# Recurrence and feed-forward on one core: output tiles of their own, more transposes by DMA, and a written order for every step

## The chip, the cores and the metric

The kernel runs on one core of a Trainium2 chip. The metric is the device time of one execution in microseconds (us). Three runs of the kernel before gave 186.01, 186.14 and 186.18 us; the median is 186.14 us.

## What is computed

The reference has two parts. The first is a recurrence with decay over 768 positions, for 4 batches x 8 heads, with head size 48. All inputs are float32.

```python
for t in range(S):
    cur = np.einsum('bhd,bhe->bhde', u[None] * kt, vt)
    y[:, :, t] = np.einsum('bhd,bhde->bhe', rt, state + cur)
    state = wt[:, :, :, None] * state + np.einsum('bhd,bhe->bhde', kt, vt)
```

The second takes y as a matrix x of 3072 rows and 384 columns and computes `h = x @ w_in` (384 x 2048), `g = max(0.01 h, h)` and `g @ w_out` (2048 x 384).

## The kernel before, in words

The 3072 rows are cut into 24 chunks of 128 positions, six for each batch. The recurrence is turned into matrix products inside a chunk, with a state carried from chunk to chunk inside a batch. Chunks 0 to 3 are done as two pairs (`pair`), whose rows are dealt out alternately so that a load moves runs of 384 bytes; the other twenty one at a time (`single`), in runs of 192 bytes.

For a single chunk the steps are these. Four loads bring w, k, r and v (192 KB each) into a quarter each of a tile `in` (L516). ACT takes the logarithm of w (`lw`, L383). PE forms its cumulative sum in PSUM (`cp`, L737) and the decay of the whole chunk (L742). DVE adds one row (`ci`, L752); ACT takes exponentials (L393). DVE or POOL multiply r and k by them and write bfloat16 (`rk`, L334). r and k are then transposed into `rkT`, in `turn`: either eight PE transposes into PSUM (L441) and two copies, or one DMA transpose issued by SP (L431). PE computes the scores (`se`, `so`, L787), DVE masks them (`m`, L459), and PE sums the part from the state (L817) and the part within the chunk (L822) into `yp`. The bonus for u is made apart: POOL multiplies r by u and by k (`ru`), DVE sums over a head (`dg`, L416), POOL multiplies v by that (`vs`). In `finish` DVE adds `yp` and `vs` into y (L490), and y is transposed into a slice of `xT`: by three PE transposes (L504) and a copy, or by a DMA transpose on SP (L496). The state goes on through an outer product (L798), a sum (L479) and a product with the decay (`sb`).

The feed-forward part works chunk by chunk on `xT`. An up group is 12 matmuls into one of two PSUM banks `hp` (L860); ACT applies the leaky function and writes a quarter of `g` (L907). A down group is 4 matmuls into a bank `op` (L928), which needs one quarter of `g` and one quarter of `w_out`. After four down groups ACT or DVE copies `op` to a tile `o` (one of four), and SP stores it (L968). The last chunk is computed in two column parts, 256 and 128 wide (L928 and L940), which are copied and stored apart (L952).

The weights come as 16 halves of 384 KB (L363), each of which is cast to bfloat16 (L329 or L331) by DVE, ACT or POOL. They pass through the same ring of 11 `in` tiles as the chunks' inputs.

The order of the work is set at build time. Each step is added to a `Plan` with an engine, a duration and its dependencies. `EARLY` ranks the steps by hand, with letters that move some to another engine; `Plan.order` then plays a schedule by priorities and gives the sequence in which instructions are issued. Every engine then works strictly in its own sequence. All loads, stores and DMA transposes are issued by SP, in one queue; only the row u is fetched by ACT. While little has arrived, PE is fed matmuls on zeros (L991).

Of the kernel before, what the change touches and what calls it, by code (L numbers as in the profile page):

```python
# [2 lines left out]

# [9 lines left out]
AX = mybir.AxisListType  # L13


class Plan:
# [23 lines left out]
    def order(self):  # L40
        n = len(self.eng)
        users = [[] for _ in range(n)]
        left = [len(d) for d in self.deps]
        for i, d in enumerate(self.deps):
            for j in d:
                users[j].append(i)
        ready_at = [0.0] * n
        start, done = [None] * n, [0.0] * n
        free = {e: 0.8 for e in self.ENGINES}
        coming = {e: [] for e in self.ENGINES}  # L50
        ready = {e: [] for e in self.ENGINES}
        dma_free = 0.0
        flying = []
        for i in range(n):
            if not left[i]:
                heapq.heappush(coming[self.eng[i]], (0.0, i))
        events = [(0.8, e) for e in self.ENGINES]
        heapq.heapify(events)
        count = 0
        while events:  # L60
            now, e = heapq.heappop(events)
            if free[e] > now + 1e-9:
                continue
            while coming[e] and coming[e][0][0] <= now + 1e-9:
                _, i = heapq.heappop(coming[e])
                heapq.heappush(ready[e], (self.pri[i], i))
            if not ready[e]:
                if coming[e]:
                    heapq.heappush(events, (coming[e][0][0], e))
                continue  # L70
            _, i = heapq.heappop(ready[e])
            start[i] = now
            count += 1
            free[e] = now + self.dur[i] * (1.8 if e == "PE" and now < 8 else 1)
            if self.wire[i] is None:
                done[i] = free[e] + self.LAT[e]
            else:

                flying = [x for x in flying if x[0] > free[e]]
                while sum(x[1] for x in flying) + self.rows[i] > 3300:  # L80
                    free[e] = max(free[e], flying.pop(0)[0])
                dma_free = max(dma_free, free[e]) + self.wire[i]
                done[i] = dma_free + 1.7
                flying.append((done[i], self.rows[i]))
            heapq.heappush(events, (free[e], e))
            for j in users[i]:
                left[j] -= 1
                same = self.eng[j] == e and self.wire[i] is None
                ready_at[j] = max(ready_at[j], free[e] if same else done[i])
                if not left[j]:  # L90
                    f = self.eng[j]
                    heapq.heappush(coming[f], (ready_at[j], j))
                    heapq.heappush(events, (max(ready_at[j], free[f]), f))
        assert count == n, (count, n)
        self.start, self.done = start, done
        return sorted(range(n), key=lambda i: (start[i], i))


class Ring:
# [7 lines left out]
    def take(self):  # L107
        self.n += 1
        k = self.n % len(self.tiles)
        old, self.steps[k] = self.steps[k], []  # L110
        return Use(self.tiles[k], old, self.steps[k])

# [14 lines left out]
def kernel(  # L127
# [24 lines left out]
    TDMA = range(12, NCH)  # L152
# [4 lines left out]
    PWIRE, WIRE, WWIRE = 1.53, 1.15, (1.12, 1.12)  # L157
# [4 lines left out]
    EARLY = """  # L162
        0 4 2 1 3 5 8 58 7 13 6 61 12 32v 36 17 11 16 22 33 120 14 21 30 19 37 18 20 24 15 59 10a 23 26
        9 27 31v 28 40 25 60 29a 38 41a 51 34 39 63 44 53 114 62 42 116 45 65a 66 118 121 64 67 122 46
        35 43 71 68 124 47 126 52 74 73 69 96 48 70 128 76 49 75p 72 136 50v 132 79 115a 78 54 91 80 81
        117 130 83 55 77p 82v 56 84a 721 119 134 92 57 85 722 723 86v 138 87 123a 93 95 725 724 97 125p
        98v 727 726 146 127p 729 99 728 88v 100 129 94 731 89 730 102 137p 140 732 733 101 735 133 148
        90 103 734 131 107 736 104 741 135p 144 109 105 742 106v 139a 142 747 108 737 147 150 110 738
        152 141p 178 743 111 153 112 748 304 744 162 113v 754 167 166 155 168 145v 749 154 753 156 750
        143p 149 739 158 163v 179 157p 755 740 759 164 756 180 160 159 182 762 760 184 209 306 745 763v  # L170
        161 185 765 764 746 151v 169 181 187 165v 751 199 761 189p 198 186 170 171 766 752 172 768 302
        173 757 208 188 174 758 192 210 200v 770 193 774 175 183a 239 194v 190 176 775 767 191a 195v 769
        211 177 196 201 779 197 202 212 237 777 780 203 214 771 224 271 778 215 204 217 781 225v 253 303
# [90 lines left out]
    with tc.manual_schedule():  # L264
# [52 lines left out]
        def step(eng, dur, fn, pri, reads=(), writes=(), deps=(), wire=None, rows=0, **alts):  # L317
# [5 lines left out]
            for x in (*reads, *writes):  # L323
                x.steps.append(i)
            return i

        def copy(e, o, i):
            if e == "ACT":
                nc.scalar.copy(out=o, in_=i)  # L329
            else:  # L330
# [697 lines left out]
```

## Time and profile before

| | |
|---|---|
| profiled execution | 186.2 us, with a span of 184.1 us |
| median of three runs | 186.14 us |
| PE busy | 175.5 us (95% of the span), 2579 matmuls |
| PE weight loads busy | 136.5 us (74%) |
| DVE busy | 121.8 us (66%), 237 instructions |
| ACT busy | 121.5 us (66%), 263 instructions |
| POOL busy | 93.4 us (51%), 129 instructions |
| DMA queue of SP and ACT | 34.22 MB in 120208 packets, 84.6% of 16 engines |
| from HBM, to HBM | 25.17 MB, 4.72 MB |
| stores of 192 KB | 23, median 3.2 us from issue to landing |
| DMA transposes of r and k | 12, median 4.2 us from issue to landing |
| DMA transposes of y | 12, median 2.6 us from issue to landing |

The profile is of one execution, so sums of its durations are to be set against its own 186.2 us. The 2.1 us beside the span lie around it. A PE that shows as busy is not a PE at its pace, since matmuls are pipelined and their ends are modelled; the distance from one group's start to the next one's is the better price. In the timeline a line gives the start, the time until the last instruction's end, engine, line, operation, tiles and count, and in brackets the idle time before it and what ended it. SPq stands for SP's queue of transfers, and PEld for the weight loads of PE. In the stretches each engine's busy time is followed by its count of instructions; the last three columns are granted clock, DMA share and GB/s.

### The profile page before, as it was taken

What the parts mean: (1) busy time and instruction counts of PE and PEld (TensorE: products, weight loads), DVE (VectorE), ACT (ScalarE), POOL (GpSimd) and SP (SyncE); (2) the same over time, 40 slices, a digit from 0 to 9 for tenths busy, and PEclk for the clock granted to TensorE, in tenths of its full rate; (3) what the DMA queues carried; (4) which work ended last, traced back from release to release, by engine and by line L of the source; (5) the groups of instructions that cost most, each with busy time, mean ns of one, the idle gap of its engine ahead of it and who ended that gap; (6) DMA issues with size and microseconds to landing.
All of it is one profiled execution on the core that took longest, in us unless ns stands there. A gap on an engine that the chain in (4) does not pass through costs nothing.

```text
span 184.1 us, 6227 instructions
## 1 busy us (share of the span) xinstructions
PE 175.5 (95%) x2579; PEld 136.5 (74%) x2583; DVE 121.8 (66%) x237; ACT 121.5 (66%) x263; POOL 93.4 (51%) x129
## 2 busy tenths in 40 slices
PE   7977799999999999999999999999999999999992
PEld 2455587877788687789687787886968777877882
DVE  2498585468679878987968768557548588755000
ACT  2784875666787887698957586766657645652660
POOL 7987582552566778789065667313516346110000
PEclk9999999999999999999999999999999999999999
DMA  6999999999999899996885997988989997641202
GB/s 150 261 282 319 348 331 275 266 180 219 221 185 232 167 234 200 227 206 151 174 155 103 135 196 152 212 166 174 191 196 192 169 183 206 162 115 33 66 4 85
DMA packets 120238, 34.62 MB, mean 188 GB/s; under 512 B 109841, under 2 KB 120210, under 8 KB 120210
## 3 DMA queue, kind: packets, MB, share of 16 engines
q1 hardware_dynamic: 120208, 34.22, 84.6%
q8 instruction: 20, 0.33, 0.7%
q14 instruction: 8, 0.07, 0.1%
q10 hardware_dynamic: 2, 0.00, 0.0%
HBM read 25.17 MB, written 4.72 MB: 162 GB/s over the span
## 4 chain that ended last, share of the span: by engine, by line
PE 82%; SPq 10%; DMA 5%; ACT 1%; issue 0%; DVE 0%
PE op L928 34%; PE hp L860 33%; SPq L363 5%; DMA in<-in_moe_w_out_dram 5%; SPq L516 4%; PE se L787 3%; PE yp L822 2%; PE cp L737 2%; PE yp L817 2%; PE yp L798 2%; PE so L441 1%; PE yp L504 1%; PE se L441 1%; PE cp L742 1%; ACT g L907 1%
## 5 line engine op out<-in xcount | busy, mean ns | idle before, releaser
L907 ACT ACTIVATE g<-hp 128x512 bf16<-128x512 f32 x96 | 56.8, 596 | 35.3 <-PE hp L860 33.4
L860 PE MATMUL hp<-xT,w_in_b 128*128 128x128 bf16 x1152 | 76.2, 219 | 1.4 <-ACT w_in_b L329 0.9
L860 PEld LDWEIGHTS <-w_in_b 128*128 128x128 bf16 x1152 | 67.4, 98 | 6.4 <-ACT w_in_b L329 1.2
L928 PE MATMUL op<-w_out_b,g 128*128 128x384 bf16 (+1 forms) x380 | 71.4, 324 | 0.2 <-ACT g L907 0.2
L928 PEld LDWEIGHTS <-g 128*128 128x128 bf16 x392 | 34.8, 98 | 17.8 <-DVE w_out_b L331 0.3
L334 POOL TENSOR_TENSOR ru<-in,ub 128x384 f32<-128x384 f32 x19 | 19.1, 1010 | 11.7 <-DMA in<-in_r_dram 8.1
L334 POOL TENSOR_TENSOR rk<-in,ek 128x384 bf16<-128x384 f32 x15 | 15.6, 1038 | 17.2 <-ACT ek L393 15.9
L334 POOL TENSOR_TENSOR vs<-in,dg 128x384 f32<-128x384 f32 x19 | 16.2, 855 | 14.2 <-DVE dg L416 11.1
L490 DVE TENSOR_TENSOR y<-yp,vs 128x384 bf16<-128x384 f32 x24 | 13.3, 554 | 13.1 <-PE yp L822 9.6
L334 POOL TENSOR_TENSOR ru<-ru,in 128x384 f32<-128x384 f32 x15 | 15.6, 1043 | 3.9 <-DMA in<-in_k_dram 2.3
L334 POOL TENSOR_TENSOR sb<-s,a 128x384 bf16<-128x384 f32 x13 | 11.3, 867 | 11.9 <-DVE s L479 5.1
L459 DVE TENSOR_TENSOR m<-se,maskb 128x512 bf16<-128x512 f32 x20 | 13.7, 684 | 3.6 <-PE so L787 3.3
L459 DVE TENSOR_TENSOR m<-so,maskb 128x512 bf16<-128x512 f32 x20 | 13.7, 684 | 3.2 <-PE so L787 3.2
L383 ACT ACTIVATE lw<-in 128x384 bf16<-128x384 f32 x24 | 12.3, 519 | 3.3 <-DMA in<-in_w_dram 3.3
L334 DVE TENSOR_TENSOR rk<-in,cp 128x384 bf16<-128x384 f32 x22 | 12.0, 547 | 3.1 <-ACT cp L393 2.1
L752 DVE TENSOR_TENSOR ci<-cp,lw 128x384 f32<-128x384 f32 x20 | 11.1, 553 | 3.8 <-PE cp L742 3.5
L416 DVE TENSOR_REDUCE dg<-ru 128x8 f32<-128x384 f32 x24 | 13.0, 544 | 0.2
L329 ACT COPY o<-op 128x384 f32<-128x384 f32 (+1 forms) x16 | 7.5, 471 | 6.5 <-PE op L928 5.1
L479 DVE TENSOR_TENSOR s<-yp,sb 128x384 f32<-128x384 f32 x14 | 7.8, 554 | 5.2 <-PE yp L798 4.3
L393 ACT ACTIVATE cp<-cp 128x384 f32<-128x384 f32 x22 | 10.5, 478 | 0.6 <-DVE ci L752 0.3
L393 ACT ACTIVATE ek<-ci 128x384 f32<-128x384 f32 x20 | 10.4, 518 | 0.4 <-DVE ci L752 0.2
L787 PE MATMUL se<-rkT 48*128 48x128 bf16 x80 | 7.9, 219 | 0.0
(125 smaller groups left out, 220.7 us busy)
## 6 DMA issues: line engine op xcount, KB each, us to landing
out_dram<-o SPq DMA_DIRECT2D x23, 192.0 KB, 3.2
in<-in_w_dram SPq DMA_DIRECT2D x20, 192.0 KB, 4.0
in<-in_r_dram SPq DMA_DIRECT2D x20, 192.0 KB, 3.8
in<-in_k_dram SPq DMA_DIRECT2D x20, 192.0 KB, 3.8
in<-in_v_dram SPq DMA_DIRECT2D x20, 192.0 KB, 3.8
in<-in_moe_w_in_dram SPq DMA_DIRECT2D x8, 384.0 KB, 7.6
in<-in_moe_w_out_dram SPq DMA_DIRECT2D x8, 384.0 KB, 7.5
in<-in_w_dram SPq DMA_DIRECT2D x2, 384.0 KB, 5.0
```

The costliest lines, as they stand in the source:

```text
L334: (nc.vector if e == "DVE" else nc.gpsimd).tensor_tensor(out=o, in0=a, in1=b, op=ALU.mult)
L363: "SP", 0.45, lambda part=part, src=src: nc.sync.dma_start(out=part, in_=src), pri,
L383: lambda: nc.scalar.activation(out=lw.t[:, :, 0:D], in_=wn.t, func=AF.Ln),
L393: "ACT", 0.5, lambda: nc.scalar.activation(out=out.t[:], in_=i, func=AF.Exp, scale=scale),
L416: lambda: nc.vector.tensor_reduce(out=dg.t[:], in_=ru.t[:], axis=AX.X, op=ALU.add),
L459: lambda par=par: nc.vector.tensor_tensor(out=m.t[:, par], in0=gt(sc[par].t), in1=mask.unsqueeze(1).to_broadcast([128, NP, 128]), op=ALU.m ...
L490: lambda: nc.vector.tensor_tensor(out=y.t[:], in0=hd(yp.t[:, 0:DM]), in1=vs.t[:], op=ALU.add),
L752: lambda: nc.vector.tensor_tensor(out=ci.t[:], in0=hd(cp.t[:, 0:DM]), in1=lw.t[:, :, 0:D], op=ALU.add),
L787: nc.tensor.matmul(gt(sc[par].t)[:, p, :], lhsT=rkT.t[q0 : q0 + D, NP + p, :], rhs=rkT.t[q0 : q0 + D, p, :], start=True, stop=True, skip_g ...
L860: nc.tensor.matmul(hp.t[:, a * N : (a + 1) * N], lhsT=w_in_b[:, t, (j + a) * 128 : (j + a + 1) * 128], rhs=xT[:, t, c0 : c0 + N], start=(a ...
L907: lambda hp=hp, g=g, j=j, J=J, N=N: nc.scalar.activation(out=g.t[:, j : j + J, 0:N], in_=hp.t[:, 0 : J * N].rearrange("p (a n) -> p a n", ...
L928: nc.tensor.matmul(t[:, 0 : n1 - n0], lhsT=g.t[:, j, off : off + 128], rhs=w_out_b[:, j, n0:n1], start=(j == 0), stop=(j == NJ - 1))
```

## The change

DMA transposes of r and k begin at chunk 9 instead of 12, and those of y at chunk 6. Weight casts of w_in get an access pattern whose outer dimension is 2 instead of 3. Outputs of chunks 4 to 23 no longer turn through four `o` tiles: chunks 0 to 3 keep one each, and the others get a quarter each of the `in` tiles 6 to 10, which the weights have left. So single chunks turn through six `in` tiles (1 to 5, and 0). Stores of chunks up to 20 rank behind the loads. Loads of single chunks and stores may be issued by ACT as well as SP; the new order has ACT issue five loads and two stores. The last chunk's down groups are regrouped: all of the 256-wide part's first three quarters, then the 128-wide part's first two, its rest at the very end. `EARLY` and the schedule by priorities go: `ORDER` lists every step once, in the sequence in which it is issued, with letters (a, v, p, s) for the engine. `Plan.order` only reads it and reckons times for the matmuls on zeros. Some reckoned durations of steps differ; they have no other effect. The core of the diff:

```diff
-    def order(self):
+    def order(self, words):
+
+        order = []
+        for word in words.split():
+            i = int(word.rstrip("avps"))
+            if word[-1] in "avps":
+                self.eng[i] = {"a": "ACT", "v": "DVE", "p": "POOL", "s": "SP"}[word[-1]]
+                self.dur[i] = self.alts[i][self.eng[i]]
+            order.append(i)
...
+    def use(self, k):
+
+        return Use(self.tiles[k], list(self.steps[k]), [])
...
-    TDMA = range(12, NCH)
+    TDMA = range(9, NCH)
+    YDMA = range(6, NCH)
+    OLATE = 21
...
-    EARLY = """
...
+    ORDER = """
...
     in_r = ring("in", 11, [128, 1536], F32)
+    pair_slots = iter((0, 1, 2, 3))
+    weight_slots = iter((4, 5, 6, 7, 8, 9, 10, 0))
+    chunk_slots = cycle((1, 2, 3, 4, 5, 0))
...
+    def out_tile(ch):
+
+        if ch < 4:
+            return o_r.take()
+        slot, i = divmod(ch - 4, 4)
+        use = in_r.use(6 + slot)
+        return View(use, use.t[:, i * DM : (i + 1) * DM])
...
+        def queue(e):
+            return nc.sync if e == "SP" else nc.scalar
...
+        def even(t, which):
+
+            return t if which else t.rearrange("p t (a f) -> p a t f", a=2)
...
-            st = in_r.take()
+            st = in_r.take(next(weight_slots))
...
-                    lambda e, dst=dst, part=part: copy(e, dst, part), CASTS, reads=[st], deps=[ld],
-                    DVE=0.8, ACT=0.84, POOL=1.2))
+                    lambda e, dst=even(dst, which), part=even(part, which): copy(e, dst, part),
+                    CASTS, reads=[st], deps=[ld], DVE=0.63, ACT=0.84, POOL=0.84))
...
-            if n in TDMA:
+            if n in YDMA:
                 xt_steps.append(step(
...
-                "SP", 0.45, lambda: nc.sync.dma_start(out=view(use), in_=src), P0 + 0.1 * i,
-                writes=[use], wire=wire, rows=1024, deps=[cums[n - AHEAD]] if n >= AHEAD else [])
+                "SP", 0.62, lambda e="SP": queue(e).dma_start(out=view(use), in_=src), P0 + 0.1 * i,
+                writes=[use], wire=wire, rows=1024, deps=[cums[n - AHEAD]] if n >= AHEAD else [],
+                **({"SP": 0.62, "ACT": 0.47} if n >= 4 else {}))
...
-            slot = in_r.take()
+            slot = in_r.take(next(chunk_slots))
...
+        def quarters(op, g, off, which):
+            for part, q in which:
+                t, n0, n1 = last_parts(op)[part]
+                for j in range(q * NJ // 4, (q + 1) * NJ // 4):
+                    nc.tensor.matmul(
+                        t[:, 0 : n1 - n0], lhsT=g.t[:, j, off : off + 128], rhs=w_out_b[:, j, n0:n1],
+                        start=(j == 0), stop=(j == NJ - 1))
...
+                    if last:
+                        quarters(op, g, off, ((0, q),) if q < 2 else ((0, 2), (1, 0), (1, 1)))
+                        return
...
-                        o = o_r.take()
...
+                        o = o_r.take() if part else out_tile(ch)
+                        s_dn = step(
+                            "PE", (0.44, 0.46)[part],
+                            lambda op=op, g=g, off=off, qs=(((0, 3),), ((1, 2), (1, 3)))[part]: quarters(op, g, off, qs),
+                            pri, reads=[g, op, side], deps=deps)
...
-                    o = o_r.take()
+                    o = out_tile(ch)
...
-                        lambda o=o, ch=ch: nc.sync.dma_start(
+                        lambda e, o=o, ch=ch: queue(e).dma_start(
                             out=rows[ch], in_=o.t[:]),
-                        5, reads=[o], deps=[s_o], wire=0.55, rows=128)
+                        5 if ch >= OLATE else 300, reads=[o], deps=[s_o], wire=0.55, rows=128, SP=0.48, ACT=0.47)
...
-        for i in plan.order():
+        for i in plan.order(ORDER):
```

## The prediction, made before the changed kernel was run

> **What bounds the kernel now.** I read the slices of the span first, then the stretches, the timeline of PE, the casts of the weights, and the chain's end.
>
> ```profile
> PE   7977799999999999999999999999999999999992
> DMA  6999999999999899996885997988989997641202
> ```
>
> PE is full from slice 7 (28 us) to the last slice. DMA is full up to about 80 us, has room after it and much at the end.
>
> ```profile
> 0.00:28.00 28.00, 22.82 (x377) 15.16 (x381) 18.01 (x45) 18.59 (x37) 21.67 (x49) 1.00 1.08 283
> 28.00:170.00 142.00, 141.82 (x2068) 112.21 (x2066) 103.26 (x191) 96.75 (x216) 71.77 (x81) 1.00 0.88 183
> ```
>
> The second column is PE: 141.82 of 142 us, while DVE, ACT and POOL have slack. A busy PE need not be a PE at its pace, so I took the pace from starts in the timeline of PE:
>
> ```profile
> 65.63 0.39 PE L441 MATMUL se<-ident,rk 128*128 128x128 bf16 x4
> 65.85 0.81 PE L928 MATMUL op<-w_out_b,g 128*128 128x384 bf16 x4
> 66.50 1.50 PE L860 MATMUL hp<-xT,w_in_b 128*128 128x128 bf16 x24
> 67.84 0.33 PE L817 MATMUL yp<-sb,rkT 128*128 128x96 bf16 x4
> ...
> 69.35 0.33 PE L504 MATMUL yp<-ident,y 128*128 128x128 bf16 x3
> 69.52 0.33 PE L928 MATMUL op<-w_out_b,g 128*128 128x384 bf16 x1
> ```
>
> From start to start: four transposes of r or k cost 0.22 us, three of y 0.17, an up group (12 matmuls) 0.67, a down group (4) 0.65. The same reading gives the scores of a chunk 0.32, the cumulative sum 0.27, the outer product 0.17, and the two parts of y 0.17 and 0.20. I put these prices on every group of PE's instruction list, leaving out the matmuls on zeros: the real work is **163.0 us** in the list of before and **160.7 us** in that of after. Clock minus work done so far is the time lost. At L737's groups before it is 15.1 us (33.3 us on the clock), 15.2 (40.3), 16.2 (90.0), 17.3 (148.6), and 17.85 when PE ends at 180.85. So 15 us are lost in the first 33 us, and then only some 0.12 us per chunk, which I take for what my prices miss. PE has no stall worth having after 33 us: the time is start-up, PE's work, and the tail.
>
> The start-up is set by weights coming in. Their casts on POOL, ACT and DVE start as the halves land, each after a wait for its DMA:
>
> ```profile
> 26.47 0.82 POOL L331 CAST w_out_b<-in 128x768 bf16<-128x768 f32 x1 [0.40 <-DMA in<-in_moe_w_out_dram]
> ```
>
> ```profile
> 27.64 0.83 ACT L329 CAST w_out_b<-in 128x768 bf16<-128x768 f32 x1 [0.59 <-DMA in<-in_moe_w_out_dram]
> 31.31 0.83 ACT L329 CAST w_out_b<-in 128x768 bf16<-128x768 f32 x1 [1.85 <-DMA in<-in_moe_w_out_dram]
> ```
>
> Others start at 28.84 (DVE), 30.11 and 33.05 (POOL), 35.91 (DVE). So a half lands each 1.17 us, and 31.31 to 33.05 and 33.05 to 35.91 hold one small load each (192 KB): 1.74 - 1.17 = 0.57, and 2.86 - 2.34 = 0.52. A small load among them costs **0.55 us**.
>
> **What the Trainium skill says.** "TensorE: Matmul & The Clock Gate", section "Wait — 56ns, not 53.3ns?", gives a warm matmul N / 2.4 GHz plus about 2.5 ns, 55.6 ns for 128 columns: the trace agrees, 0.67 us / 12 = 56 ns. "DMA: Bandwidth & Descriptors", section "Issuing engines are not separate DMA queues", says that transfers issued by ACT run on the same 16 engines and save only issue time; before, ACT issues one tiny transfer, so the trace is silent. "VectorE: DVE Perf Modes", section "What auto-detection actually checks", wants outermost dimensions that are both even for the fast copy of one source: the trace agrees, 0.95 us for the DVE cast of w_in with an outer 3, and 0.56 for w_out with an outer 4 (once 0.83).
>
> **The change, part by part.**
>
> *Transposes off PE.* r and k of chunks 9, 10, 11: 3 x 2 x 0.22 = 1.32 us. y of chunks 6 to 11: 6 x 0.17 = 1.02 us. All lie in the full stretch: **-2.34 us**. With them go their PSUM copies (6 at 0.41 to 0.59, 6 at 0.36 to 0.48 us on ACT and DVE), nothing on the path.
>
> *What takes their place.* Nine DMA transposes more on SP. An issue holds SP for 1.2 us (y) or 1.2 to 3.1 (r and k, median 1.54), and landing takes a median of 2.6 and 4.2 us from the issue. Nothing waits long if PE has other work. In PE's list of after, y to its first up group is 5.4 to 10.0 us apart for chunks 9 to 20 and 5.9 to 7.3 for chunks 6 to 8 (needed: DVE 0.55, landing 2.6, some 0.2 of latency: 3.3). Cumulative sum to scores is 8.8 us at the least (chunk 23) and 9.5 to 16 otherwise; needed are 0.25, 0.55 (DVE), 0.5 and 0.5 (ACT), 0.55 and 0.65 to 1.04 (products), then 4.2, in all about 7.5 us. Before has 8.1 at chunk 23 and does not stall. Cost 0, with about 1 to 2 us of cover at chunks 11, 12, 17, 18, 22 and 23; a landing of 5.5 (the longest seen) would cost some tenths.
>
> *Stores behind loads, a tile each.* Before the last load 13 stores are issued instead of 19, so 6 x 192 KB make room for nine transposes (3 x 256 KB, 6 x 96 KB). DMA's share of 0.88 between 28 and 170 us stays about the same. Six stores now stand in SP just ahead of the transpose of chunk 22: at 0.35 to 0.55 each some 3 us of queue, for which the list leaves 16 us from cumulative sum to scores. Cost 0. The loads of chunks 4 on turn in six buffers instead of eleven; each load is held until the fifth chunk before has its sum anyway. Cost 0; if late readers held a buffer, a load would slip by the time of one bonus product on POOL (1.0 us), under the same cover.
>
> *Start-up order.* This has a price. The first down group now comes after 12.0 us of work (before: 14.5), and its two halves of w_out are SP's transfers 16 and 17 (before: 18 and 19). Transfer 17 landed at 26.47 before, with the same bytes ahead. So the cast ends at about 27.1, and the first down group can start some 2 us before the old 29.47. But work moved behind it too, so what counts is the loss. Following each wait with the rows of before: the two halves for up group 1 land at 18.5 and 19.64, and POOL's second cast ends near 20.5; ACT's copy of y (0.48), of keys (0.58) and g (0.60 each) follow one another, and the first down group starts at about 27.4, a loss of 15.4. Then two loads of chunk 5 issued by ACT (right after the fifth and sixth g, near 27.2 and 28.0) and one of chunk 4 go ahead of w_out's last halves. Second quarter: 26.47 + 3 x 1.17 + 2 x 0.55 = 31.1, POOL 0.83 and latency: 32.0, where PE wants it at 31.4. Third quarter: 31.1 + 0.55 + 3 x 1.17 = 35.1, ACT 0.83: 36.05, at 19.8 us of work: a loss of **16.25 us**. Fourth: 36.3, POOL to 37.2, work 21.96: no wait. Before had lost 15.15 there: **+1.1 us**. Bounds: -0.3 (ACT's loads fall behind the weights, 2 x 0.55, and a cast or two is quicker) to +1.9 (each of the three small loads costs 0.93 us, the pace between 40 and 80 us at 207 GB/s, and a g is late by 0.5).
>
> *Even casts.* One DVE cast of w_in falls from 0.95 to about 0.56; ACT and POOL keep 0.83. It waits for a landing and has slack: 0.
>
> *ACT issues five loads and two stores.* At about 0.5 us each, 3.5 us of ACT that had 45 us idle in the full stretch; behind each are g's, and PE has two hp banks. In the lists every transfer waits for the one issued eight before it, on whichever queue; those before ACT's loads are old. Cost 0, at worst one g late by 1 us or so each time.
>
> *Tail.* Before, PE ends at 180.85, DVE's copy takes 0.29, two stores are issued one after the other, and the span ends 3.25 us after PE. After, the 128 KB store is ready 1.7 us early, the 64 KB one stands alone on SP, and ACT sends another of 192 KB. I take 3.0: **-0.25**, bounds -0.5 and +0.3.
>
> **Sum.** -2.34 + 1.1 - 0.25 = -1.5 us. The profiled execution took 186.2 (span 184.1 and 2.1 around it), 0.06 above the median of 186.14. So 186.2 - 1.5 = **184.7 us**.
>
> **Rivals.** (a) *The start-up loses nothing more*: ACT's loads fall in a hole, and the whole of PE's saving shows: 186.2 - 2.34 - 0.25 = 183.6; down to 182.9 where the earlier down groups fill time that was lost. For it: DMA moved 266 to 348 GB/s in this stage, so there is some room. (b) *The saving is hidden or given back*: the weights take all of 1.9 us, or one late transpose 1 us, and 186.2 stands. Against: PE is full after 33 us. (c) *Slower: SP's queue becomes the bound.* 33 transposes instead of 24 stand in order with the loads, and each that waits for its product holds up all behind it. Place: chunks 11, 12, 17, 18, 22, 23, where cover is 1 to 2 us. Price: an issue of 3.1 instead of 1.5 and a landing of 5.5 instead of 4.2 make 2.9 us, 1.4 beyond a cover of 1.5. Two such come to 2.8: 184.7 + 2.8 = 187.5. It decides from 1.9 us of PE stalls on. For it: SP waited for products of DVE and POOL up to 3.6 us at a time before; against: that never stalled PE.
>
> **Chances.** Below 183.2: 0.06. Rival (a), 183.2 to 184.2: 0.24. The forecast, 184.2 to 185.75: 0.45. Rival (b), 185.75 to 186.5: 0.09. Rival (c): 0.16. About 0.2% (0.37 us) is what measuring this kernel can tell from no change. Faster 0.75, same 0.09, slower 0.16. The range leaves out 0.06 below and some 0.14 above: 183.2 to 186.6.
>
> **What would show it.** Right: 42 fewer transposes on PE, PE full from about 36 us on, the loss near 16.2 us at the fourth w_out quarter and growing by 0.12 per chunk, POOL and ACT waiting for w_out until about 31, 35 and 36 us, span near 182.6. Wrong: scores (L791) or up groups (L864) waiting for a DMA in mid-span, ACT idle behind its own loads, g late, or a tail above 3.5 us.

## The result, and the profile after

The changed kernel takes **191.85 us** (median of four runs, 190.54 to 193.25), the kernel before 186.16 (186.01 to 186.41) in the same comparison: a ratio of 1.031, with a 95% interval from 1.023 to 1.038. It is slower by 5.7 us. In some of the kernels below, single executions lie more than 1.5% above the fastest of the same kernel; the medians count them, the ratios leave them out. The forecast of 184.7 and its range to 186.6 were wrong; the nearest rival was (c), slower through SP's queue, at 187.5. The profiled execution of the changed kernel took 192.25 us, with a span of 189.9.

The slices of the span, after (each column is 4.75 us):

```profile
PE   7988779899999999999997899999999899999992
PEclk9999999999999999999999699999999999999999
DMA  6999999998996898999999968989999998941302
```

PE, full before from slice 7 on, now has a hole in slices 22 and 23 (100 to 109 us), with a lower granted clock in the second, and a small one in slice 32 (147 to 152 us). With the prices of the forecast put on the 160.7 us of real work in after's list, the loss (clock minus work) reads at the cumulative sums, L741: 17.82 us at chunk 5 (43.05 on the clock), 19.14 at chunk 14 (89.41), 21.79 at chunk 15 (105.11), 23.43 at chunk 16 (113.00), 24.04 at chunk 21, 24.99 at chunk 22 (150.34), and 25.65 when PE ends at 186.31. Against before's losses (15.21 at chunk 5, 17.85 at the end) the span's 5.8 us come out as follows: PE's work -2.34, start-up +2.61, from there to PE's end +5.19 (4.05 of it from chunk 14's sum to chunk 16's, 0.83 from chunk 21's to chunk 22's), tail +0.34 (3.59 us from PE's end to the span's, before 3.25).

The chain of what ended last, after, through the hole (start, us, what):

```profile
96.88 2.39 SPq L434
99.27 0.04 issue
99.31 0.58 SPq L519
...
99.99 4.52 DMA in<-in_w_dram
104.51 0.02 issue
104.53 0.53 ACT lw L386
105.06 0.04 issue
105.11 0.32 PE cp L741
105.43 0.08 PE cp L746 x4
105.51 2.09 PE hp L864 x24
```

PE waited for the sum of chunk 15 (L741), that for ACT's logarithm, that for the load of w, and the load for its turn on SP, behind the transposes. Two up groups then took 2.09 us, where 1.34 is usual: the second part of the loss, 1.64 us, is a lower clock. This is one execution: in the profile of stores_last, below, every engine has the same sequence up to 106.30 us, and yet the loss at chunk 15 is 1.9 us smaller and the clock doesn't fall. What two profiles differ by at this place is therefore no sure sign of an edit. SP's queue in the timeline, after:

```profile
89.00 2.71 SPq L499 DMA_TRANSPOSE xT<-y  x1
91.75 0.58 SPq L519 DMA_DIRECT2D in<-in_v_dram  x1
92.44 1.72 SPq L434 DMA_TRANSPOSE rkT<-rk  x1
94.20 0.58 SPq L519 DMA_DIRECT2D in<-in_k_dram  x1
94.89 1.20 SPq L499 DMA_TRANSPOSE xT<-y  x1
96.13 0.58 SPq L519 DMA_DIRECT2D in<-in_r_dram  x1
96.88 2.39 SPq L434 DMA_TRANSPOSE rkT<-rk  x1
99.31 0.58 SPq L519 DMA_DIRECT2D in<-in_k_dram  x1
99.99 0.53 SPq L519 DMA_DIRECT2D in<-in_w_dram  x1
```

and before, in the same stretch:

```profile
84.90 1.36 SPq L431 DMA_TRANSPOSE rkT<-rk  x1
86.31 0.57 SPq L516 DMA_DIRECT2D in<-in_r_dram  x1
86.93 0.63 SPq L516 DMA_DIRECT2D in<-in_k_dram  x1
89.39 0.36 SPq L968 DMA_DIRECT2D out_dram<-o  x1
89.79 0.43 SPq L516 DMA_DIRECT2D in<-in_k_dram  x1
91.50 1.24 SPq L431 DMA_TRANSPOSE rkT<-rk  x1
```

Before has holes of 1.8 and 1.3 us ahead of 89.39 and 91.50; after has none. Added up over the timeline (gaps under 0.2 us closed), SP is taken 11.3 of the 20 us from 80 to 100 before, and 20.0 of 20 after. Each transpose of y of chunks 8 to 13 is issued 1.1 to 2.7 us after its y is done. The DMA engines are busier there too. The stretch from 80 to 100 us, before and then after (the last three columns are granted clock, DMA share, GB/s):

```profile
80.00:100.00 20.00, 20.00 (x300) 15.91 (x298) 16.03 (x31) 15.80 (x40) 12.34 (x15) 1.00 0.77 157
```

```profile
80.00:100.00 20.00, 19.80 (x291) 15.69 (x290) 16.20 (x33) 12.79 (x29) 9.98 (x12) 1.00 1.07 159
```

The same 157 to 159 GB/s, but a share of 1.07 in place of 0.77. (The share adds up the time that packets took, and these times overlap: it reaches 1.35 between 104 and 106 us. So a share of 1 is no ceiling.) The DMA queues of after (q1 is SP's; q10 is ACT's, with its seven transfers of 192 KB):

```profile
q1 hardware_dynamic: 120384, 34.22, 86.9%
q10 hardware_dynamic: 5490, 1.38, 3.3%
```

90.2% of 189.9 us is 171.3 us of packet time; before it was 84.6% of 184.1, 155.7 us. The nine transposes add 1.38 MB (4%), and the packet time grows by 15.6 us (10%). The trace's packets tell the two parts of it apart by size, for only transposes have packets of 256 bytes (1024 of them for r and k, 384 for y). Their sum over 16 engines goes from 25.0 to 34.3 us: +9.3 are more transposes. The 192-byte packets of the loads are as many as before and take 16.9 ns each in place of 15.7: +5.7 us are the same loads, slowed. From 80 to 100 us they take 20.9 ns.

The start-up, after, on POOL, ACT and DVE:

```profile
33.63 0.83 POOL L330 CAST w_out_b<-in 128x768 bf16<-128x768 f32 x1 [1.78 <-DMA in<-in_moe_w_out_dram]
```

```profile
36.74 0.83 ACT L328 CAST w_out_b<-in 128x768 bf16<-128x768 f32 x1 [1.76 <-DMA in<-in_moe_w_out_dram]
```

```profile
24.27 1.00 DVE L330 CAST w_in_b<-in 128x768 bf16<-128x768 f32 x1 [1.16 <-DMA in<-in_moe_w_in_dram]
25.18 0.54 DVE L482 TENSOR_TENSOR s<-se,sb 128x384 f32<-128x384 f32 x1
```

The cast of w_out's third quarter begins at 36.74, with the landing; forecast 35.1. The casts before it were at 31.02 and 33.63, so the two small loads that ACT sent stretched the landings by 33.63 - 31.02 - 1.17 = 1.44 and 36.74 - 33.63 - 2.34 = 0.77 us, where I had 0.55 each. And DVE waited for a half of w_in with its sums of the state behind it; PE waited 1.2 us for such a sum until 27.25.

### The profile page after: what moved, and what is told of

Same layout as the page of the kernel before. It is cut to its first block, busy times and chain, and to the rows that moved or that the text cites. A ratio compares the mean times of both kernels' runs of the same rounds, so it can differ in the third digit from the quotient of the medians.

```text
span 189.9 us, 6143 instructions
## 1 busy us (share of the span) xinstructions
PE 177.7 (94%) x2546; PEld 137.4 (72%) x2546; DVE 119.2 (63%) x229; ACT 114.4 (60%) x250; POOL 100.6 (53%) x138
## 3 DMA queue, kind: packets, MB, share of 16 engines
q10 hardware_dynamic: 5490, 1.38, 3.3%
## 4 chain that ended last, share of the span: by engine, by line
PE 67%; DMA 14%; SPq 10%; DVE 3%; POOL 2%; ACT 1%; issue 1%; DVEq 0%
PE hp L864 27%; PE op L944 27%; SPq L519 5%; DMA in<-in_moe_w_in_dram 4%; DMA in<-in_moe_w_out_dram 4%; SPq L366 4%; PE se L791 3%; DMA xT<-y 3%; DMA in<-in_w_dram 2%; PE yp L826 2%; PE cp L741 2%; PE yp L821 1%; SPq L434 1%; PE yp L802 1%; PE op L885 1%
## 5 line engine op out<-in xcount | busy, mean ns | idle before, releaser
L864 PE MATMUL hp<-xT,w_in_b 128*128 128x128 bf16 x1152 | 77.5, 221 | 2.2 <-POOL w_in_b L330 1.0
L864 PEld LDWEIGHTS <-w_in_b 128*128 128x128 bf16 x1152 | 68.7, 99 | 8.6 <-issue 2.1
L944 PE MATMUL op<-w_out_b,g 128*128 128x384 bf16 x368 | 70.6, 329 | 0.9 <-ACT w_out_b L328 0.9
L944 PEld LDWEIGHTS <-g 128*128 128x128 bf16 x368 | 32.9, 98 | 18.4 <-ACT w_out_b L328 1.1
L333 POOL TENSOR_TENSOR ru<-in,ub 128x384 f32<-128x384 f32 x23 | 24.2, 1056 | 5.7 <-DMA in<-in_r_dram 3.5
L333 POOL TENSOR_TENSOR rk<-in,ek 128x384 bf16<-128x384 f32 x14 | 14.3, 1023 | 13.0 <-ACT ek L396 8.7
L333 POOL TENSOR_TENSOR ru<-ru,in 128x384 f32<-128x384 f32 x17 | 17.0, 1005 | 7.4 <-DMA in<-in_k_dram 7.0
L333 POOL TENSOR_TENSOR sb<-s,a 128x384 bf16<-128x384 f32 x12 | 10.4, 863 | 8.9 <-DVE s L482 5.6
L330 POOL CAST vb<-in 128x384 bf16<-128x384 f32 x11 | 5.7, 516 | 8.3 <-PE so L791 7.0
L993 PE MATMUL op<-zeros 128*128 128x512 bf16 (+1 forms) x24 | 8.8, 463 | 1.2 <-DVE zeros L298 1.2
```

The source lines that it names most:

```text
L333: (nc.vector if e == "DVE" else nc.gpsimd).tensor_tensor(out=o, in0=a, in1=b, op=ALU.mult)
L864: nc.tensor.matmul(hp.t[:, a * N : (a + 1) * N], lhsT=w_in_b[:, t, (j + a) * 128 : (j + a + 1) * 128], rhs=xT[:, t, c0 : c0 + N], start=(a ...
L944: nc.tensor.matmul(op.t[:, 0:DM], lhsT=g.t[:, j, off : off + 128], rhs=w_out_b[:, j, :], start=(j == 0), stop=(j == NJ - 1))
L993: nc.tensor.matmul(op_r.tiles[1][:, 0:n], lhsT=zeros[:, 0:128], rhs=zeros[:, 0:n], start=True, stop=True)
```

## The experiments

**Theory A**: the nine transposes fill SP's queue, in which loads and transposes stand in order; something is late for PE. **Theory B**: they fill the 16 DMA engines, whoever issues. **Theory C**: it is the order of particular steps, and not room. Where an edit moves steps in the order, it does so with a helper: `moved(ORDER, x, y)` puts step x ahead of step y, `given(ORDER, letter, ...)` gives steps to an engine. In "the order of the kernel before", its sequence of steps is written out.

**The transposes alone.** On the kernel before, in its own order:

```diff
-    TDMA = range(12, NCH)
+    TDMA = range(9, NCH)
+    YDMA = range(9, NCH)
```

> The kernel before, its buffers and its order of steps kept, with r and k of chunks 9, 10, 11 and y of chunks 9, 10, 11 transposed by DMA on SP instead of by PE. Theory A (the forecast's steps: PE's work falls by 3 x 0.44 + 3 x 0.17 = 1.83 us, and six transposes more on SP cost nothing): 184.3 us. Theory B (SP's queue or the DMA engines have no room for them): 186.2 us or more, with PE waiting for a load or a transpose between 60 and 100 us.

Measured: 190.97 us (189.29 to 193.13; before 186.31). The two executions that a ratio would count took 189.29 and 189.36, the second of them profiled: +3.0 us. The waits of PE from 80 to 110 us in it, and two of them in the timeline:

```profile
PE hp L843 <- DMA xT<-y: 3.8, 3, 1.7
PE se L770 <- DMA rkT<-rk: 0.7, 1, 0.7
```

```profile
84.35 0.84 PE L843 MATMUL hp<-xT,w_in_b 128*128 128x128 bf16 x12 [1.62 <-DMA xT<-y]
101.03 0.84 PE L843 MATMUL hp<-xT,w_in_b 128*128 128x128 bf16 x12 [1.71 <-DMA xT<-y]
```

PE's loss goes from 16.23 us at chunk 12 to 21.74 at chunk 16; before and after that stretch it runs as in the kernel before. Six transposes, nothing else changed, turn a gain of 1.8 us into a loss of 3.0. SP is taken 20.0 of 20 us from 80 to 100, the DMA share is 0.98, and packet time rises from 155.7 to 165.1 us. A and B both fit. But so does C in part, for this order was made for PE's own transposes. y of chunks 9, 10 and 11 is done at 80.45, 88.67 and 95.72, and PE is ready for the up group that waits at 82.73, 93.44 and 99.31: it has 2.3, 4.8 and 3.6 us of other work. In after y and the first up group of its chunk are 4.9, 5.8 and 7.7 us apart. The transposes came 3.9, 5.2 and 5.3 us after their y: 1.0, 2.3 and 1.2 us in SP's queue, then 2.8, 3.0 and 4.0 to landing. The 2.3 us at chunk 9 are too few even for the usual landing of 2.6. So the 3.0 us are the price of six transposes in this order, not of transposes as such. The way back, on the changed kernel (`TDMA` and `YDMA` from 12, its order kept):

> The changed kernel with the nine transposes given back to PE (DMA from chunk 12 for both), the rest of its order kept. PE's work rises by 2.34 us. Theory A (the nine transposes on SP caused the wait near 105 us): that wait of 4.1 us goes, 191.85 + 2.34 - 4.1 = 190.1 us. Theory B (the order of loads or the buffers caused it, whatever the transposes): 194.2 us, with PE still waiting for the w of chunk 15 near 107 us.

Measured: 198.71 us. PE's loss grows from chunk 9 on (18.6) to chunk 15 (26.4), through waits for y, copies and g of up to 1.3 us. That order leaves PE's own transposes no room, so this run says nothing on A or B.

**SP's time without bytes.** On the kernel before, at the places of the six transposes (`SPOTS`):

```diff
+            for _ in range(SPOTS.count(i) * 3):
+                n = next(spare)
+                nc.sync.dma_start(out=junk[:, 8 * n : 8 * n + 8], in_=u[0:1, 8 * (n % 6) : 8 * (n % 6) + 8])
```

> The kernel before, its order kept (all its transposes by PE stay), with 18 extra transfers of 32 bytes issued by SP, three at each of the six places where the run with r, k and y of chunks 9 to 11 by DMA had its six transposes; their data is not used. They take SP about 18 x 0.45 = 8 us, as six transposes did (9.3 us), but move next to nothing. Theory A (SP's issue time is the bound that the transposes hit): PE waits as in the run with six transposes, some 3 to 6 us, 189 to 192. Theory B (the DMA engines are the bound): within 0.5 us of before, 186.3.

Measured: 186.24 us, ratio 0.9996 (0.998 to 1.002). SP was taken 20.0 of 20 us from 80 to 100, the DMA share there was 0.98, and PE lost no more than before. These are the two numbers of the run with six transposes: a full queue and a high share don't by themselves make anything late. The 18 took some 6.4 us, less than I had reckoned. Twice as many (`* 6`):

> The run before_sp18 with twice as many tiny transfers: 36, six at each of the six places. At the 0.35 us that each took there they hold SP for some 12.6 us, more than six transposes (9.3 us) and more than the 9.6 us that SP had free between 80 and 110 us. Theory B (SP's time is not what counts as long as the bytes get through): 186.3, within 0.5. Theory A: here at last PE waits, 188 or more.

Measured: 189.62 us, ratio 1.016 (1.013 to 1.019). PE waited 1.2 us for DVE and 2.0 us for the logarithm of a w that was late, and its clock fell after the second. Its stretch from 80 to 100 us, in which the engines have room:

```profile
80.00:100.00 20.00, 18.76 (x279) 14.85 (x277) 14.49 (x29) 14.55 (x35) 11.48 (x14) 1.00 0.75 160
```

So SP's queue can make PE wait at a DMA share of 0.75; in this order the point lies between 6.4 and some 11.5 us of added time. Part of that is not issuing: SP also stood 1.7 and 1.4 us for an earlier transfer to land, since each transfer waits for the one issued eight before it, and the 36 take up such turns too. (The execution profiled, 191.55 us, is the slowest of its four.)

**Bytes without SP's time.** On the kernel before, ten loads of 192 KB by ACT at the same places (two at four of them):

```diff
+                nc.scalar.dma_start(
+                    out=junk[n % 4][:].rearrange("p (h d) -> p h d", h=H),
+                    in_=v[0, :, 0:L, :].rearrange("h p d -> p h d"))
```

> The kernel before, its order kept (all its transposes by PE stay), with ten extra loads of 192 KB issued by ACT at the same six places; their data is not used. At the pace of 0.93 us for one they take the 16 engines 9.3 us, as the six transposes did (9.4 us of packet time more in that run), and take nothing of SP. Theory B (the DMA engines are the bound): PE waits 3 to 6 us, 189 to 192. Theory A (SP's issue time): within 0.5 us of before, or up to 1.5 us more where ACT is held at its own issues and a g is late.

Measured: 190.42 us, ratio 1.014 (1.010 to 1.019). It looks like B, but in the execution profiled (192.85 us) the chain of waits runs through ACT:

```profile
86.30 5.18 DMA in<-in_v_dram
91.48 0.02 issue
91.50 0.55 ACTq L976
92.05 0.05 issue
92.10 0.52 ACT ek L380
```

ACT stood at its own transfer until an earlier one of SP had landed, with exponentials and g behind it. The run shows a price of loads on ACT; it doesn't decide for B.

**Fewer bytes with all transposes.** v from chunk 10 on is cut, on the changed kernel and on the run with six transposes:

```diff
+            def rows_of(i):
+                return 16 if i == 3 and n >= 10 else L
-                load_in(use, src[b, :, t0 : t0 + L, :].rearrange("h p d -> p h d"), P0, i, n,
+                load_in(use, src[b, :, t0 : t0 + rows_of(i), :].rearrange("h p d -> p h d"), P0, i, n,
```

> The changed kernel with the loads of v from chunk 10 on cut to 16 of 128 positions, so that the other positions keep old data: a part of the input is left out. Each such load is still issued by SP, but moves 24 KB in place of 192, an eighth. Theory A (SP's issue time): loads and transposes still hold SP as long, PE still waits near 105 us, 191 to 192. Theory B (the DMA engines are full): a quarter of the loads' bytes is gone, the holds of SP shorten too, and the waits of PE from 100 us on go: 187 to 188.

> The run before_t9y9 (the kernel before with six transposes more by DMA) with the loads of v from chunk 10 on cut to 16 of 128 positions: a part of the input is left out. Every transfer is still issued by SP, the transposes as before; some 6 us of the 16 engines' time are freed before 100 us. Theory B (the DMA engines are the bound that the transposes hit): the 5.9 us that PE lost at chunks 13 to 16 fall below 1 us, and PE's 1.83 us less work shows: 184.4 (184.0 to 185.2). Theory A (SP's queue, with its order and its holds of 1.2 to 2.5 us): still 189 to 192.

Measured: 188.56 (ratio 1.010, 1.006 to 1.014) and 188.34 us (1.012, 1.007 to 1.016). The first lies between what A and B gave, with 3.3 of 5.7 us won; the second is nearer to A, with 1.0 of the 3.0 us won. What remains, remains at the same places in the two executions profiled (190.56 and 188.86 us). In the second, PE still waits for transposes of y, 4.4 us in all, with the engines at 0.89:

```profile
PE hp L846 <- DMA xT<-y: 4.4, 3, 2.5
```

```profile
80.00:100.00 20.00, 16.12 (x228) 12.24 (x225) 12.78 (x23) 13.56 (x33) 11.97 (x15) 1.00 0.89 169
```

B alone falls; bytes matter, but are not the whole. In the second run the rest is three waits for y of the chunks behind which this order has little other work.

**SP relieved.** On the changed kernel:

```diff
+    ORDER = given(ORDER, "a", "406", "405", "434", "433", "462", "461", "490", "489", "518", "517", "544", "543")
```

> The changed kernel with the loads of k and w of chunks 13 to 18 (12 of 192 KB) issued by ACT instead of SP, at the same places of the order; all transfers and their bytes stay. Theory A (the time that SP needs to issue is short: loads and transposes stand back to back in its queue from 70 to 107 us, and nine transposes of 1.2 to 2.4 us each are more than the 9.6 us that SP had free there before): SP gains 12 x 0.6 = 7 us, the waits of PE at chunks 15 and 16 go, loss 19.2 in place of 23.5 at chunk 17, and 187.9 us. Theory B (the 16 DMA engines are full, whoever issues): landings stay late, 191 to 192. Worse than 192 would mean that ACT is held up at its own loads and that g is late.

Measured: 191.5 us, ratio 1.025 (1.020 to 1.030): nothing won. The chain at chunk 15 shows what took the place of SP:

```profile
101.42 1.38 ACTq L525
102.81 0.05 issue
102.85 0.60 ACT g L925
103.45 0.42 ACTq L525
103.87 0.04 issue
103.91 0.32 PE cp L747
```

From 99.0 us on ACT issues five loads, at 0.4 to 1.4 us each, and g and the logarithm come behind them. SP is taken 17.0 us of the 20 from 80 to 100 and 13.9 of the next 20, against 20.0 and 18.0 in after, and nothing is won by it. Work taken from one queue stands ahead of something else in the queue that gets it. With the shorter v as well:

> The changed kernel with both reliefs at once: k and w of chunks 13 to 18 issued by ACT, and v from chunk 10 on cut to 16 of 128 positions (a part of the input is left out). If SP and the DMA engines are the only two limits near 105 us: the waits at chunks 15 and 16 go (loss 19.3 at chunk 16 against 20.6 with the first relief alone and 21.4 with the second) and the time is 187.0. If PE still waits there, something else is late: ACT behind its own issues, or the order itself.

Measured: 188.46 us (1.013, 1.010 to 1.016), as with the shorter v alone; PE still waits 1.4 us at chunk 15, for ACT.

**The order.** w of chunk 15 ahead of the transpose of chunk 12:

```diff
+    ORDER = moved(ORDER, "461", "392")
```

> The changed kernel with one step moved: SP issues the load of w for chunk 15 ahead of the DMA transpose of r and k of chunk 12 instead of behind those of chunks 12, 13 and 14 and of y of chunks 10 and 11. Theory A (order: that one load stood behind transposes in SP's queue, and the other loads have slack): the wait of PE near 105 us and the low clock after it go, about 4.1 us, so 187.8 us (187.0 to 188.7). Theory B (capacity: SP or the DMA engines are full from 60 to 110 us, and another load is late in its stead): no more than 1 us is won, 190.8 to 192.

Measured: 192.03 us (1.026, 1.018 to 1.033). PE no longer waits for w, and the loss at chunk 16 is 20.2 us in place of 23.4. That is what C says, but stores_last, with w where after has it, reads 19.9 there. 2.0 us come back as one wait for the transpose of r and k near the end, and the time is the same. So C is not shown by this run. Start-up: both ACT loads behind the weights; in the second run also the DVE cast given to ACT, `given(ORDER, "a", "125")`:

```diff
+    ORDER = given(ORDER, "s", "178", "179")
+    ORDER = moved(ORDER, "178", "149")
+    ORDER = moved(ORDER, "179", "149")
```

> The changed kernel with the two loads of chunk 5 that ACT issued among the last weights given back to SP, behind all the weights. In the trace these two stretched the landings of w_out by 1.44 and 0.77 us. Theory A (the weights' landings set the start-up): the last halves land some 2 us earlier, the start-up loss falls from 17.8 to about 16.7 us or less, and the time by 1 us or more, to 190.8 or below. Theory B (the start-up is set by the order of steps on POOL and DVE, which made PE wait before 28 us): no change within 0.4 us, about 191.85. Slower only if chunk 5 is then late for PE.

> The run with the weights first once more (both loads of chunk 5 by SP behind the weights), and one cast of w_in (third quarter, second half) given from DVE to ACT, so that DVE's sums of the state do not stand behind it. Theory A (an engine that waits in order for a weight held up DVE's sums, and so PE's scores, by 1.2 us near 27 us): the loss at chunk 5 falls from 17.1 to about 15.9 us, and the time by 1.2 us from 190.3 to 189.1. Theory B (what is won there is waited for at the next weight): loss at chunk 5 stays near 17, 190.3.

Measured: 190.31 (1.022, 1.017 to 1.026) and 191.92 us (1.026, 1.017 to 1.035). The intervals overlap that of after (1.023 to 1.038), so no gain is shown. The loss at chunk 5 is 17.1 and 17.3 us in place of 17.8; w_out is no longer waited for. In the runs that leave the start-up as it is, this loss reads 17.2 to 17.8, so that even this gain is small against their spread, and the cast given to ACT wins nothing that can be seen. The whole start-up in the order of the kernel before:

> The changed kernel, its buffers and transposes kept, with the order of the kernel before for all steps up to the cumulative sum of chunk 5 (loads of chunks 6 on excepted), and its own order from there. Theory 1 (the start-up's order costs what the two traces show, 17.8 us lost at chunk 5 against 15.2): the loss at chunk 5 is 15.2 to 15.6, and the time 189.3. Theory 2 (what is won at the start is lost again where the loads come late): loss at chunk 5 as said, but the wait at chunk 15 grows by as much, and 191 to 192.

Measured: 192.37 us; the ratio, of its two faster executions (191.86 and 189.3), is 1.023 (1.018 to 1.029), which overlaps that of after. In the profile (192.88 us) the loss at chunk 5 is 15.4 us, 2.4 better. At chunk 15 PE waits for w again, 2.0 us, and the sum comes at 103.90 on the clock against 105.11: there half of the gain is left. Two more waits, of 1.1 and 1.8 us, follow. This is what theory 2 says, for this execution; no gain in time is shown. w of chunk 15, the weights first, the cast and the twelve loads by ACT, all in one:

> All of these edits at once on the changed kernel: weights first, the cast given to ACT, the load of w for chunk 15 ahead of the transpose of chunk 12, and the twelve loads issued by ACT. If the waits add up and SP's issue time was the bound: loss 15.9 us at chunk 5 and about 18.5 at chunk 23, PE's end near 179.5 us and the time 185.2 us, below the 186.3 of the kernel before. If the DMA engines are the bound: 188 or more.

Measured: 190.05 us (1.019, 1.014 to 1.023); PE waits at chunk 15 for ACT (1.1 us), at 146 us for y (1.15) and at 165 us for r and k (1.5). Then the stores, which so far I had left:

```diff
+    for step in ("867", "839", "881", "909", "895", "825", "923", "811", "797", "749", "951", "758"):
+        ORDER = moved(ORDER, step, "1021")
+    for step in ("853", "937", "783", "979", "761", "746"):
+        ORDER = moved(ORDER, step, "679")
```

> The changed kernel with the 18 stores that SP issues among loads and transposes from 107 us on moved behind them: six ahead of the transpose of y of chunk 22, twelve behind that of chunk 23. SP has some 8 us less in its queue between 107 and 166 us and the DMA engines some 8 to 10 us less. Theory A (SP's queue and its transfers together set when loads and transposes come): the waits at chunks 21 and 22 (about 1 us in the profile) and any wait ahead of the last chunk go, that at chunk 15 stays, since no store stands ahead of it: 190.5 us. Theory B (the order of the stores does not matter): 191.9. If the stores then make the tail longer: up to 193.

Measured: **188.25 us** (1.016, 1.010 to 1.021), the largest step of any single edit, -3.6 us. In its profile PE waits for nothing after 103.2 us, and the loss grows by 0.12 us per chunk from 19.9 at chunk 15 to 20.9 at chunk 23, where after went from 21.8 to 25.2. But the first store that moves stood at 106.30 us, so what lies ahead of it can't be the edit's doing. PE waited 0.7 us at chunk 15 there, in place of 1.6, and had no fall of the clock after it. Of the 4.2 us between the two profiles' spans 3.5 are there at chunk 16, and only 0.8 come between it and PE's end. So the time won is clear, its cause isn't: the stores behind the rest are worth some 0.8 us by these two profiles, and why the earlier wait was shorter is open. Everything in order at once (the start-up of before, w of chunk 15, the stores):

> The changed kernel with all orders mended at once and nothing else: the start-up of the kernel before, w of chunk 15 ahead of the transpose of chunk 12, the stores behind the transposes. If each wait seen so far was one of order: loss 15.4 at chunk 5, 17 to 18 at chunk 16, some 19 at the end of PE; 160.7 + 19 + 3.6 + 2.1 = 185.4 us, faster than both kernels. If SP's queue and the DMA engines simply have no room for 33 transposes, whatever the order: another load or transpose is late in mid-span, 187.5 to 190.

Measured: **187.3 us** (186.47 to 188.7; ratio 1.006, 1.004 to 1.009). The same steps and transposes as after, 4.5 of 5.7 us gone; not faster than before. Its largest waits of PE:

```profile
PE op L962 <- ACT g L937: 1.4, 1, 1.4
...
PE se L809 <- DMA rkT<-rk: 0.9, 1, 0.9
```

The first is at the seam where the two orders meet (44 us), my own doing; the second is a transpose at 91.8 us. A version without the seam was not tried. Of the 5.7 us, then, 4.5 were won by order alone (theory C), while SP stays taken 20.0 of 20 us from 80 to 100, at a DMA share of 1.10. Which of the three edits won how much is not shown: the start-up and w of chunk 15 alone show no gain, and of the stores' 3.6 us only 0.8 can be placed.

**Room for a few.** The kernel before, with transposes of r, k and y of chunk 11, and in the second run with those of r and k of chunks 10 and 11 (`TDMA` from 10, `YDMA` from 12):

```diff
+    TDMA = range(11, NCH)
+    YDMA = range(11, NCH)
```

> The kernel before, its order kept, with r and k of chunk 11 and y of chunk 11 alone transposed by DMA: two transposes more, in the stretch from 80 to 100 us where SP was taken only 11 of 20 us and the DMA engines 0.77. PE's work falls by 0.44 + 0.17 = 0.61 us. Theory A and B alike, if the room is what counts: 185.7 us, faster than before by 0.3%. If a transpose is late for PE however much room there is (its latency of 4 us): 186.3 or more.

> The kernel before, its order kept, with r and k of chunks 10 and 11 transposed by DMA and y as before: two transposes more, PE's work less by 0.88 us. Theory B (room in the DMA engines counts: 4.6 us of their time were free from 80 to 100 us, and two transposes take some 3 to 4 us): they fit, 185.4 us. If there is no room for that of chunk 10, issued near 75 us where the engines were at 0.97: 186.2 to 187.

Measured: 185.95 us (six runs, ratio 0.999, 0.996 to 1.002) and 186.35 (fourteen runs, 1.000, 0.999 to 1.002). Two transposes fit without harm, though that of y of chunk 11 landed 3.3 us after its y, just as PE came to it; of the 0.6 and 0.9 us that PE saves nothing can be told from no change. No version was shown to beat the kernel before.

## Why the prediction was wrong, by its steps

*What takes their place: cost 0.* This step failed, and the runs show its cost: after the start-up PE lost 5.2 us more than before, most of it in waits for a load of w (1.6 us) and a transpose of y (0.8) that came late through SP's queue, and in the fall of the clock (1.6). The step asked, for each transpose, whether the distance in PE's list covers one landing as measured before, and never asked what nine of them do to SP's queue and to other landings. A landing of y's transposes took a median of 3.3 us from the issue and not 2.6, after up to 2.7 us in the queue; the load of w of chunk 15 stood behind four transposes and then took 4.5 us to land. SP's part in numbers: 3 issues of 1.5 us and 6 of 1.2 are 11.7 us. SP had 8.7 us free between 80 and 100 us and 0.9 in the 40 us before; five of the nine were issued between 59 and 78 us. The engines' part: "6 x 192 KB make room" and "DMA's share stays about the same" were reckoned by bytes. By before's packets a store of 192 KB takes 0.56 us of the 16 engines, a transpose of r and k 1.52 and one of y 0.57. So six stores give 3.4 us and nine transposes take 8.0.

These sums show a risk, not a price: before_sp18 filled the same stretch of SP's queue, at a share of 0.98, and lost nothing. The price depends on the order: six transposes in an order with little other work behind y cost 3.0 us (before_t9y9), two cost nothing, and all nine in a better order leave 1.2 us of the 5.7 (orders_mended). SP's queue alone can do harm (before_sp36), fewer bytes win 1.0 and 3.3 us in the two runs with the shorter v, and neither relief alone suffices. How the loss divides among queue, bytes and order is not settled: fewer bytes also shorten SP's issues and landings.

*Stores behind loads: cost 0.* It looked at six stores before chunk 22, but 18 stand among loads and transposes from 106 us on. Put behind them, the kernel took 3.6 us less (stores_last); 0.8 us of that can be placed behind the first store moved. So the cost was not 0, but its size is open.

*Start-up: +1.1.* The mechanism was right, its terms too small: +2.6 us at chunk 5. The small loads by ACT stretched the landings by 1.44 and 0.77 us, not 0.55 each, and DVE's in-order wait for a weight (1.2 us) was not seen; giving that cast away won nothing, so its share is not shown. And the start-up may not simply add to the sum: mended alone it won nothing that can be told (after_before_start), for PE then waited longer at chunk 15.

*Transposes off PE: -2.34* holds as PE's work: with the same prices the loss grows by about 0.12 us per chunk wherever PE doesn't wait, in after as in before. *Even casts: 0* holds in sum, but DVE's cast took 1.00 us and not 0.56, and it had no slack: it is the cast that DVE's sums stood behind. *ACT issuing: 0* holds as far as a g goes: PE waited 0.2 us for one in all; with nineteen transfers, ACT became the queue (act_loads). *Tail: -0.25* was wrong by 0.6: +0.34.

*Rival (c)* named the right mechanism, an in-order SP queue, and a point of 1.9 us of PE stalls from which it decides. Its place was wrong: not the scores that wait for their transposes at the chunks with little cover, but first a load that stood behind four transposes. Its price, 2.8 us for two late transposes, lacked the fall of the clock. I gave it 0.16, because SP's waits had never stalled PE before; that was with nine transposes fewer in the queue.

## What to carry to other kernels

Before work is moved to a shared in-order queue, add up that queue's time and the transfer engines' packet time by stretch, by packets and not by bytes. Where that leaves nothing free, each item's turn in the queue has to be added to its latency before it is set against the work that is to cover it; a latency that fits one item says nothing on nine. A full queue alone is no proof of a loss. And two profiles of one kernel can differ by as much as an edit does: what lies ahead of the edit's first instruction tells by how much. A transfer nobody waits for, such as a store, is best kept behind the ones that are waited for, and giving loads to a second engine only helps if that engine has nothing in order behind them.

## What the runs showed of the hardware that I had not expected

- A DMA transpose costs the engines little more for its bytes than a load in short runs, but holds its queue longer. The Trainium skill, "Advanced Engine Details and Errata", section "X-Bar Transpose (TRN2)", calls them as fast as regular DMAs and expects 350 to 400 GB/s, about 90% of a plain copy. By the packets of before, over all 16 engines, transposes move 173 GB/s and loads in runs of 192 bytes 196; after, 166 and 182. So the ratio agrees, 88 to 91%, and the rate is half of what the page expects; the measurement decides.
- PE's clock can fall soon after a wait that is much shorter than 3.4 us. The Trainium skill, "TensorE: Matmul & The Clock Gate", section "Part 1: The HAM clock gate", speaks of an idle window of about 3.4 us and of half rate. Half rate agrees, in stretches of 2 us of after, behind the hole of 1.63 us that ends at 105.11 (granted clock is the third number from the end):

```profile
104.00:106.00 2.00, 0.89 (x16) 0.83 (x16) 1.60 (x4) 1.01 (x2) 0.00 (x0) 0.98 1.35 207
106.00:108.00 2.00, 2.00 (x18) 1.69 (x16) 0.77 (x2) 0.96 (x2) 0.00 (x0) 0.50 1.33 211
108.00:110.00 2.00, 2.00 (x20) 1.57 (x19) 0.00 (x0) 1.19 (x4) 0.99 (x1) 0.66 1.17 265
110.00:112.00 2.00, 2.00 (x30) 1.54 (x28) 1.31 (x3) 0.90 (x3) 0.66 (x1) 1.00 0.24 41
```

  It began about 1 us after work had resumed, lasted 3.4 us and cost 1.64 us. The clock also fell for 3.4 us after waits of 2.0 us in before_sp36 and after_before_start and of 2.3 in before_dma10. But it did not fall after waits of 1.7 us in weights_first and short_v, of 2.0 in w15_early and of 2.5 in t9y9_short_v. So the length of the wait alone doesn't decide, and what does is open here. Where the clock falls, a wait of 1.6 us costs about twice its length, and kernels whose PE waits spread more: 190.5 to 193.3 us here, 186.0 to 186.4 before.
- The cast of w_in with even outer dimensions took DVE 1.00 us (one instance), as with an odd one before (0.95). The condition that the forecast took from the Trainium skill, "VectorE: DVE Perf Modes", was met and did not suffice here; why was not tried.
- A transfer of 32 bytes holds SP for 0.25 us (median of 36), a load for at least 0.37 and some 0.6 to 0.75 in the median (after), a transpose for at least 1.18.
